# Stores of dK, dV and three weight gradients issued by ScalarE instead of GpSimd, in a decode layer's forward and backward pass

## The chip, the cores and the metric

The kernel runs on one core of a Trainium2 chip. The metric is the device time of one execution in microseconds (us); lower is better. A core has five engines that run instruction streams of their own: TensorE (PE in the profile), VectorE (DVE), ScalarE (ACT), GpSimd (POOL) and SyncE (SP). The last three can issue DMAs. An engine works through its stream in order, and an instruction that waits for a semaphore holds up all that stand behind it on its engine.

## The reference

One decode step of a transformer layer and all its gradients. There is one token of width 448. Attention has 16 heads of 256 over 8 groups of keys and values, and looks at the last 4096 of 32768 cached positions.

```
q = layernorm(x) @ wq;  k, v = the caches' last W = 4096 rows
p = softmax(q k^T / 16);  h = x + (p v) @ wo
g = layernorm(h) @ w_gate;  u = layernorm(h) @ w_up
out = h + (g * u) @ w_down
outputs: out, dx, dK, dV, dWq, dWo, dWg, dWu, dWd   (vjp with grad_out)
```

dK and dV have the shape of the whole caches, 8 x 32768 x 256 in bf16 each. All but the last 4096 rows of a group are zero, and these zeros must be written: 112 transfers of 2 MB.

## The kernel before

**Transfers.** SP loads `wq` and the first K window and then issues the 112 zero transfers (line 95, "the fills" below, numbered 1 to 112 in SP's order). Each writes the tile `zeros` to 2048 KB of `out_2` or `out_3`. GpSimd issues everything else: the loads of K and V windows (line 72, 2048 KB each), of `wo`, `w_gate`, `w_up`, `w_down` and again `wq`, and all stores of results.

**Stages.** First, for each group g of 8: scores, softmax and moments (forward attention). Then the output projection, layer norm and the gated feed-forward part, forward and backward (lines 388 to 434), which needs `w_up` as its last load. Then `dh_bc` (line 439, a ScalarE copy) and the gradient of the attention's output (line 442). Then the backward loop over g (line 551). For each g VectorE and ScalarE turn V, by transposes, into `dp`, and 16 chunks of two matmuls each (line 593) are cast from PSUM into the two 2 MB buffers `stg[0]` (dV, by ScalarE) and `stg[1]` (dK, by VectorE); line 598 stores both. There are five such buffers, `STG`, used in turn, so that a buffer of group g is free when a store of two or three groups earlier has landed.

**Weight gradients.** `outer` (line 469) multiplies rows on VectorE into a home buffer and stores it (line 474). It is called for dWg and dWu (`width` 896, 1568 KB each) right after the feed-forward backward, for dWd (`width` 448, so rows of 896 bytes, 1568 KB, home `Rt`), for dWo in two parts of 1792 KB (`width` 448, homes `Rt` and a slot of `S`), and for dWq in two parts of 2048 and 1536 KB (`width` 2048, after line 515 has reduced the reloaded `wq`). `Rt` is used in turn for dWu, the `w_down` load (line 490), dWd, the first part of dWo and the reloaded `wq`, and each of them waits until the store before it has left it.

**What sets the order.** The kernel is written in a tile language, and its planner puts the instructions of each engine in order and adds the semaphore waits. Every DMA of a hardware queue (SP, and ScalarE where it issues any) gets one of eight completion semaphores, the lanes, round and round in the planner's order over both engines; GpSimd's DMAs have eight lanes of their own. A DMA whose lane was used before waits, at issue, until the lane's DMA before it has landed. In the kernel before SP alone uses the hardware lanes: fill 50, for instance, waits for fill 42, and so on to the end, so that eight fills are under way at any time.

Of the kernel before, what the change touches and what calls it, by code (L numbers as in the profile page):

```python
# [13 lines left out]
D = 448  # L14
# [4 lines left out]
W = 4096  # L19
T = 32  # L20
F = 1792
FC = 14
Sk = 32768
# [19 lines left out]
def kernel(  # L43
        ctx, tc, A_x, A_k_cache, A_v_cache, A_wq, A_wo, B_x, B_w_gate, B_w_up, B_w_down, grad_out,
           out_0, out_1, out_2, out_3, out_4, out_5, out_6, out_7, out_8):
    nc = tc.nc
    V_, S_, P_ = nc.vector, nc.scalar, nc.tensor
    FILL = nc.sync
    IO = nc.gpsimd

    const = ctx.enter_context(tc.tile_pool(name="const", bufs=1))
    small = ctx.enter_context(tc.tile_pool(name="small", bufs=2))
# [12 lines left out]
    def slot_kv(k):  # L65
        return S[:, k, :].rearrange("p (t d) -> p t d", d=Dh)
# [4 lines left out]
    def load_window(dst, cache, g, q=None):  # L71
        (q or IO).dma_start(out=dst, in_=cache[0, g, Sk - W:, :].rearrange("(p t) d -> p t d", t=T))

# [3 lines left out]
    def load_V(g):  # L77
        load_window(Vw[g], A_v_cache, g)

    def flat_rows(w):  # L80
        return w.rearrange("a b -> (a b)").rearrange("(p x) -> p x", p=128)


    x_bf = const.tile([1, D], bf16, tag="rowa", name="x_bf")
    IO.dma_start(out=x_bf[:], in_=A_x.rearrange("a b d -> (a b) d"))
    go_bf = const.tile([1, D], bf16, tag="rowb", name="go_bf")
    IO.dma_start(out=go_bf[:], in_=grad_out.rearrange("a b d -> (a b) d"))
    wq_sb = S[:, 1:3, :].rearrange("p a b -> p (a b)")[:, 0:NI * HQ]
# [10 lines left out]
    wd0 = S[:, 3, 0:FC * D].rearrange("p (c n) -> p c n", n=D)  # L99
    IO.dma_start(out=wd0, in_=B_w_down.rearrange("(c p) n -> p c n", p=128))  # L100

# [109 lines left out]
    def evac(out, in_):  # L211
        if evac_ctr[0] % 2 == 0:
            S_.copy(out=out, in_=in_)  # L213
        else:
            V_.tensor_copy(out=out, in_=in_)  # L215
        evac_ctr[0] += 1
# [68 lines left out]
    def softmax(g):  # L285
        s = sT[g]
        pmax = small.tile([128, 2], f32, tag="pmax")
        V_.reduce_max(out=pmax[:], in_=s[:].rearrange("p t h -> p h t"), axis=AX)
        mt = ps.tile([2, 128], f32, tag="tmp", bufs=1)
        P_.transpose(mt[:], pmax[:], ident_f[:])  # L290
        gmax = small.tile([2, 1], f32, tag="gmax")
        V_.reduce_max(out=gmax[:], in_=mt[:], axis=AX)
        gd = small.tile([2, 2], f32, tag="gd")
        V_.tensor_scalar(out=gd[:], in0=ident_f[0:2, 0:2], scalar1=gmax[:, 0:1], scalar2=-SCALE, op0=ALU.mult, op1=ALU.mult)
        nb = ps.tile([128, 2], f32, tag="tmp", bufs=1)
        P_.matmul(nb[:], lhsT=ones_f[0:2, :], rhs=gd[:], start=True, stop=True)
        nbias = small.tile([128, 2], f32, tag="nbias")
        V_.tensor_copy(out=nbias[:], in_=nb[:])
        e = small.tile([128, T, 2], f32, tag="e_f")
        sums = small.tile([128, 2], f32, tag="psums")  # L300
        for h in range(2):
            S_.activation(out=e[:, :, h], in_=s[:, :, h], func=ACT.Exp, bias=nbias[:, h:h + 1], scale=SCALE, accum_out=sums[:, h:h + 1])
        rs = small.tile([128, 2], f32, tag="rsum")
        V_.reciprocal(out=rs[:], in_=total(sums[:], 2)[:])
        pf = small.tile([128, T, 2], f32, tag="p_f")
        V_.tensor_tensor(out=pf[:], in0=e[:], in1=rs[:].unsqueeze(1).to_broadcast([128, T, 2]), op=ALU.mult)
        V_.tensor_copy(out=pT_all[:, g], in_=pf[:])
        p_f[g] = pf
# [52 lines left out]
    for g in range(G):  # L361
# [6 lines left out]
        if g == 7:  # L368
            load_V(7)
            IO.dma_start(out=woA, in_=wo_v[:, 0:16, :])  # L370
        softmax(g)
# [3 lines left out]
        if g == 0:  # L375

            t = ps.tile([128, D], f32, tag="tmp", bufs=1)
            P_.matmul(t[:], lhsT=ones_bf[0:1, :], rhs=go_bf[:], start=True, stop=True)
            S_.copy(out=dh2_bc[:], in_=t[:])
            for c in range(FC):  # L380
                V_.tensor_tensor_reduce(out=wd0[:, c, :], in0=wd0[:, c, :], in1=dh2_bc[:], scale=1.0, scalar=0.0,  # L381
                                        op0=ALU.mult, op1=ALU.add, accum_out=d_hh[:, c:c + 1])
    IO.dma_start(out=woB, in_=wo_v[:, 16:32, :])
    IO.dma_start(out=wg_sb, in_=flat_rows(B_w_gate))
# [84 lines left out]
    def outer(dst, n0, n1, src, scal, width, home):  # L469

        sb = home[:, 0:(n1 - n0) * width].rearrange("p (n c) -> p n c", c=width)
        for n in range(n0, n1):
            V_.tensor_scalar(out=sb[:, n - n0, :], in0=src(n), scalar1=scal[:, n:n + 1], scalar2=None, op0=ALU.mult)
        IO.dma_start(out=dst[:, n0:n1, :], in_=sb)

    o4 = flat_rows(out_4).rearrange("p (i c) -> p i c", i=NI)
    o5 = out_5.rearrange("(b p) n -> p b n", p=128)
# [34 lines left out]
    def dxn_part(home, i0, i1):  # L512
        w = wq2(home, i0, i1)
        for i in range(i0, i1):
            V_.tensor_tensor_reduce(out=w[:, i - i0, :], in0=w[:, i - i0, :], in1=dq_bc[:, i % 2, :], scale=1.0, scalar=0.0,  # L515
                                    op0=ALU.mult, op1=ALU.add, accum_out=Pq[:, i:i + 1])
        outer(o4, i0, i1, lambda n: dq_bc[:, n % 2, :], xf1, HQ, home)

    def dx_out():
# [6 lines left out]

    side = {
        0: [lambda: outer(o6, 0, NI, lambda i: bc2[0][:, i % 2, :], xf2, HF, wg_sb),
            lambda: outer(o7, 0, NI, lambda i: bc2[1][:, i % 2, :], xf2, HF, wu_sb), load_wd],
        1: [ffn_out],  # L530
        2: [lambda: outer(o8, 0, FC, lambda n: dh2_bc[:], hh, D, Rt)],
# [13 lines left out]
    def vt_buf():  # L545
        k = vt_ctr[0] % 2
        vt_ctr[0] += 1
        return VTb[:, k, :].rearrange("p (i h c) -> p i h c", i=4, h=2)

    kt_buf = vt_buf  # L550
    for g in range(G):
        if g in V_AGAIN:
            Vw[g] = slot_kv(V_AGAIN[g])
        dp = bps.tile([128, T, 2], f32, tag="dp")
        for q in range(8):
            tr = ps.tile([128, 4, 2, 128], bf16, tag="tr", bufs=2)
            for i in range(4):
                for dh in range(2):
                    P_.transpose(tr[:, i, dh, :], Vw[g][:, 4 * q + i, dh * 128:(dh + 1) * 128], ident_bf[:])  # L559
            xt = vt_buf()  # L560
            evac(xt, tr[:])
            for i in range(4):
                for dh in range(2):
                    P_.matmul(dp[:, 4 * q + i, :], lhsT=xt[:, i, dh, :], rhs=doT[:, 4 * g + dh:4 * g + dh + 3:2],  # L564
                              start=(dh == 0), stop=(dh == 1))
        for again, sl in V_AGAIN.items():
            if sl == g:
                load_window(slot_kv(sl), A_v_cache, again)
        pds = small.tile([128, T, 4], bf16, tag="pds")
        V_.tensor_copy(out=pds[:, :, 0:2], in_=pT_all[:, g])  # L570
        df = small.tile([128, T, 2], f32, tag="df")
        V_.tensor_tensor(out=df[:], in0=dp[:], in1=delta[:, 2 * g:2 * g + 2].unsqueeze(1).to_broadcast([128, T, 2]), op=ALU.subtract)
        V_.tensor_tensor(out=pds[:, :, 2:4], in0=df[:], in1=pT_all[:, g], op=ALU.mult)
        r_ps = ps.tile([128, 128], bf16, tag="tmp", bufs=1)
        P_.transpose(r_ps[:], pds[:].rearrange("p t r -> p (t r)"), ident_bf[:])
        rows = rowb[:, g % 2]
        V_.tensor_tensor(out=rows, in0=r_ps[:].unsqueeze(1).to_broadcast([128, 8, 128]), in1=mrow[:].unsqueeze(2).to_broadcast([128, 8, 128]), op=ALU.mult)
        R_ps = ps.tile([128, 2 * Dh], f32, tag="tmp", bufs=1)
        for k, (E, rr) in enumerate(((Ed, do_rows), (Eq, q_rows))):
            ex = small.tile([H, 32, 4], bf16, tag="ex")  # L580
            V_.tensor_copy(out=ex[:], in_=E[:, g, :].unsqueeze(1).to_broadcast([H, 32, 4]))
            P_.matmul(R_ps[:, k * Dh:(k + 1) * Dh], lhsT=ex[:].rearrange("h a r -> h (a r)"), rhs=rr[:], start=True, stop=True)
        R = small.tile([128, 2 * Dh], bf16, tag="R")
        S_.copy(out=R[:], in_=R_ps[:])
        sv = slot_kv(STG[(2 * g) % 5])
        sk = slot_kv(STG[(2 * g + 1) % 5])
        stg = [sv, sk]
        for c in range(T // 2):
            d_ps = bps.tile([128, 2, 2, Dh], f32, tag="d2", bufs=2)
            for i in range(2):  # L590
                t = 2 * c + i
                k, a = t // 8, t % 8
                P_.matmul(d_ps[:, i, :, :].rearrange("p w d -> p (w d)"), lhsT=rows[32 * k:32 * k + 32, a, :], rhs=R[32 * k:32 * k + 32, :],  # L593
                          start=True, stop=True)
            for w in range(2):
                evac(stg[w][:, 2 * c:2 * c + 2, :], d_ps[:, :, w, :])
        for w, o in ((0, out_3), (1, out_2)):
            IO.dma_start(out=o[0, g, Sk - W:, :].rearrange("(p t) d -> p t d", t=T), in_=stg[w])
        for job in side[g]:
            job()  # L600

# [29 lines left out]
```

## Time and profile before

| | us |
|---|---|
| median of 3 runs (813.37 to 813.43) | 813.39 |
| profiled execution, whole | 813.5 |
| profiled execution, span of the instructions | 811.7 |
| busy in the span: PE | 490.7 |
| busy: DVE | 388.0 |
| busy: ACT | 164.7 |
| busy: POOL | 37.4 |

336.57 MB are moved by DMA in the span, 415 GB/s on average. By queue: 240.66 MB on the hardware queue of SP (70.4% of the 16 DMA engines' time), 95.13 MB on the software queue of GpSimd (27.9%). Of the 280.59 MB written to memory, 235 MB are zeros.

The profile counts time from the start of the span. In a row of the timeline the columns are start, length in time, engine, line, operation, output and inputs, and how many instructions were merged (x49). What stands in brackets is the engine's idle time just before, and what ended it. "PEclk" is the clock that TensorE was granted, as a share of full speed.

### The profile page before, as it was taken

How to read it: one execution, taken by the hardware profiler on the slowest of the kernel's cores; microseconds unless marked ns; L12 is line 12 of the kernel's file. 1: busy time of each engine (PE TensorE's matmuls, PEld its weight loads, DVE VectorE, ACT ScalarE, POOL GpSimd, SP SyncE). 2: the span in 40 equal slices, each digit the busy share in tenths (PEclk: the TensorE clock that was granted, in tenths of full speed). 3: DMA queues.
4: the chain of work that ended last, by engine and by line, in shares of the span. 5: the costliest groups of instructions: out<-in, count | busy, mean ns of one | idle time of the engine just before them, and what ended most of it. 6: DMA issues, size and time to landing. Idle time of an engine off the chain costs nothing.

```text
span 811.7 us, 12304 instructions
## 1 busy us (share of the span) xinstructions
PE 490.7 (60%) x4950; PEld 285.9 (35%) x4991; DVE 388.0 (48%) x1179; ACT 164.7 (20%) x261; POOL 37.4 (5%) x67
## 2 busy tenths in 40 slices
PE   3795956797978839252359999958996200170000
PEld 3664653555655525030336444412551000110000
DVE  4276834665656636028754555548554133550000
ACT  0311020202112000001024535534553100040000
POOL 3000000000000000000100001001101000000000
PEclk9987887887979879655555555555555555555555
DMA  9999999999999999999999999999999999999992
GB/s 376 409 427 428 427 428 430 428 428 425 426 427 425 428 410 422 427 424 434 427 421 427 430 427 414 427 423 405 427 418 426 402 428 416 430 431 430 430 423 97
DMA packets 25385, 336.57 MB, mean 415 GB/s; under 512 B 2720, under 2 KB 2768, under 8 KB 5488
## 3 DMA queue, kind: packets, MB, share of 16 engines
q1 hardware_dynamic: 16416, 240.66, 70.4%
q0 software_dynamic: 8912, 95.13, 27.9%
q8 instruction: 39, 0.64, 0.3%
q14 instruction: 18, 0.15, 0.0%
HBM read 55.18 MB, written 280.59 MB: 414 GB/s over the span
## 4 chain that ended last, share of the span: by engine, by line
issue 38%; PE 20%; DMA 14%; DVE 10%; another core or an unknown queue 6%; ACT 2%; POOL 1%; POOLq 0%; SPq 0%; DVEq 0%; ACTq 0%
PE MT L324 5%; DMA out_dram<-S 4%; DMA Rt<-in_B_w_up_dram 4%; PE d_ps L593 3%; DMA S<-in_A_k_cache_dram 3%; PE tr L559 2%; DVE S L442 2%; DMA S<-in_A_v_cache_dram 2%; PE tr L268 2%; PE acc L331 1%; DVE Rt L515 1%; DVE S L381 1%; DVE Rt L430 1%; DVE S L515 1%
## 5 line engine op out<-in xcount | busy, mean ns | idle before, releaser
L593 PE MATMUL d_ps<-R,Mt 32*128 32x512 bf16 x256 | 124.8, 612 | 57.0 <-DVE S L215 56.3
L324 PE MATMUL MT<-Rt,S 128*128 128x512 bf16 x471 | 150.5, 399 | 0.1
L320 DVE TENSOR_SCALAR Rt<-S,pf 128x256 bf16<-128x256 bf16 x512 | 120.4, 285 | 55.8 <-PE acc L331 39.2
L215 DVE CAST S<-d_ps 128x512 bf16<-128x512 f32 x128 | 87.9, 690 | 70.8 <-ACT S L213 64.5
L213 ACT CAST S<-d_ps 128x512 bf16<-128x512 f32 x128 | 75.0, 586 | 131.6 <-PE d_ps L593 130.2
L327 PEld LDWEIGHTS <-S 128*128 128x128 bf16 x512 | 50.3, 100 | 77.1 <-DMA S<-in_A_v_cache_dram 13.6
L268 PE MATMUL tr<-ident_bf,S 128*128 128x128 bf16 x512 | 50.7, 251 | 39.1 <-DMA S<-in_A_k_cache_dram 32.0
L559 PE MATMUL tr<-ident_bf,S 128*128 128x128 bf16 x512 | 69.0, 305 | 1.2 <-ACT Mt L213 1.2
L331 PE MATMUL acc<-ones_bf,Rt 128*128 128x1 bf16 x1024 | 63.2, 164 | 1.6 <-issue 1.5
L593 PEld LDWEIGHTS <-Mt 32*128 32x128 bf16 x256 | 22.7, 113 | 111.8 <-issue 110.4
L327 PE MATMUL acc<-pT_all,S 128*128 128x2 bf16 x512 | 49.3, 165 | 16.2 <-DMA S<-in_A_v_cache_dram 13.3
L213 ACT COPY Rt<-tr 128x1024 bf16<-128x1024 bf16 x32 | 32.4, 1012 | 126.7 <-PE tr L268 76.2
L559 PEld LDWEIGHTS <-S 128*128 128x128 bf16 x512 | 48.1, 135 | 25.4 <-issue 25.4
L268 PEld LDWEIGHTS <-S 128*128 128x128 bf16 x512 | 37.4, 112 | 40.9 <-DMA S<-in_A_k_cache_dram 32.6
L331 PEld LDWEIGHTS <-Rt 128*128 128x128 bf16 x1024 | 47.1, 97 | 6.2 <-issue 6.1
L213 ACT COPY Mt<-tr 128x1024 bf16<-128x1024 bf16 x32 | 32.4, 1013 | 23.5 <-PE tr L559 22.2
L215 DVE COPY Mt<-tr 128x1024 bf16<-128x1024 bf16 x32 | 22.0, 687 | 22.5 <-PE tr L559 18.9
L324 PEld LDWEIGHTS <-S 128*128 128x128 bf16 x512 | 32.5, 98 | 0.0
L168 PE MATMUL t<-st,ones_f 128*128 128x2 f32 x4 | 1.2, 364 | 48.6 <-DVE st L199 48.6
L215 DVE COPY Rt<-tr 128x1024 bf16<-128x1024 bf16 x32 | 21.9, 686 | 17.0 <-PE tr L268 15.6
L564 PEld LDWEIGHTS <-Mt 128*128 128x128 bf16 x512 | 21.1, 109 | 24.7 <-issue 10.9
L343 ACT COPY Rt<-kb 128x512 f32<-128x512 f32 x8 | 4.7, 585 | 120.2 <-PE kb L341 100.2
(189 smaller groups left out, 435.6 us busy)
## 6 DMA issues: line engine op xcount, KB each, us to landing
out_dram<-zeros SPq DMA_DIRECT2D x112, 2048.0 KB, 51.9
out_dram<-S POOLq DMA_DIRECT2D x16, 2048.0 KB, 29.1
S<-in_A_v_cache_dram POOLq DMA_DIRECT2D x10, 2048.0 KB, 41.7
S<-in_A_k_cache_dram POOLq DMA_DIRECT2D x7, 2048.0 KB, 27.5
S<-in_A_wq_dram SPq DMA_DIRECT2D x1, 3584.0 KB, 12.9
S<-in_A_wo_dram POOLq DMA_DIRECT2D x2, 1792.0 KB, 30.9
out_dram<-Rt POOLq DMA_DIRECT2D x2, 1568.0 KB, 32.9
S<-in_A_k_cache_dram SPq DMA_DIRECT2D x1, 2048.0 KB, 23.2
```

The lines of the kernel that those rows point to most:

```text
L213: S_.copy(out=out, in_=in_)
L215: V_.tensor_copy(out=out, in_=in_)
L268: P_.transpose(tr[:, i, dh, :], Xw[:, 4 * q + i, dh * 128:(dh + 1) * 128], ident_bf[:])
L320: V_.tensor_scalar(out=pk[:, i, h, :], in0=K[:, t, :], scalar1=pf[:, t, h:h + 1], scalar2=None, op0=ALU.mult)
L324: P_.matmul(MT[:, hf, :], lhsT=Vv[:, t, hf * 128:(hf + 1) * 128], rhs=pk[:, i, :, :].rearrange("p h d -> p (h d)"), start=(t == 0), stop=( ...
L327: P_.matmul(acc[:, 2 * hf:2 * hf + 2], lhsT=Vv[:, t, hf * 128:(hf + 1) * 128], rhs=pT_all[:, g, t, :], start=(t == 0 and hf == 0), stop=(t ...
L331: P_.matmul(acc[:, 4 + 2 * h + dk:5 + 2 * h + dk], lhsT=pk[:, i, h, dk * 128:(dk + 1) * 128], rhs=ones_bf[:, 0:1], start=False, stop=(t == ...
L442: V_.tensor_tensor_reduce(out=wo_b(b), in0=wo_b(b), in1=dh_bc[:], scale=1.0, scalar=0.0, op0=ALU.mult, op1=ALU.add, accum_out=doT_f[:, b:b ...
L515: V_.tensor_tensor_reduce(out=w[:, i - i0, :], in0=w[:, i - i0, :], in1=dq_bc[:, i % 2, :], scale=1.0, scalar=0.0, op0=ALU.mult, op1=ALU.a ...
L559: P_.transpose(tr[:, i, dh, :], Vw[g][:, 4 * q + i, dh * 128:(dh + 1) * 128], ident_bf[:])
L564: P_.matmul(dp[:, 4 * q + i, :], lhsT=xt[:, i, dh, :], rhs=doT[:, 4 * g + dh:4 * g + dh + 3:2], start=(dh == 0), stop=(dh == 1))
L593: P_.matmul(d_ps[:, i, :, :].rearrange("p w d -> p (w d)"), lhsT=rows[32 * k:32 * k + 32, a, :], rhs=R[32 * k:32 * k + 32, :], start=True, ...
```

## The change

A third name, `ST`, for ScalarE's DMA queue. Of the stores, those of dK and dV (16 of 2048 KB), of dWg and dWu and of the two parts of dWq now are issued by ScalarE. The stores with rows of 896 bytes (dWd and both parts of dWo), the two small outputs and all of GpSimd's loads stay on GpSimd. Nothing is changed in what is computed.

```
@@ -47,6 +47,7 @@
     FILL = nc.sync
     IO = nc.gpsimd
+    ST = nc.scalar
@@ -471,7 +472,7 @@
         for n in range(n0, n1):
             V_.tensor_scalar(out=sb[:, n - n0, :], in0=src(n), scalar1=scal[:, n:n + 1], scalar2=None, op0=ALU.mult)
-        IO.dma_start(out=dst[:, n0:n1, :], in_=sb)
+        (IO if width == D else ST).dma_start(out=dst[:, n0:n1, :], in_=sb)
@@ -595,7 +596,7 @@
         for w, o in ((0, out_3), (1, out_2)):
-            IO.dma_start(out=o[0, g, Sk - W:, :].rearrange("(p t) d -> p t d", t=T), in_=stg[w])
+            ST.dma_start(out=o[0, g, Sk - W:, :].rearrange("(p t) d -> p t d", t=T), in_=stg[w])
```

The planner's order changes with it, and the built program shows how. The 20 ScalarE stores and the fills now take turns on the same eight hardware lanes. So some fills wait for a store (dV0 and dK0 are the stores of group 0, and so on):

```
fill    50   52   58   59   64   66   68   71     75   79   82   83   88   92   94
waits   dWg  dWu  dV0  dK0  dK1  dV2  dK2  dWq b  dK3  dK4  dV5  dK5  dK6  dV7  dK7
```

All other fills wait for an earlier fill. A ScalarE store in turn waits for the fill, or the store, before it on its lane: dV1 for fill 52, dV2 for 56, dV3 for 63, dV4 for 67, dV6 for 76, dK6 for 77, dV7 for 80. SP's order of the fills and, up to the last casts of group 0, the order of PE and VectorE are those of before. After that VectorE's order differs: all 14 multiplications of dWd now follow group 0's last cast in one run, and the first ten of dWo, which overwrite dWd in `Rt`, stand before the casts of group 1 (before the change: among those of group 3). The reduction of the first part of `wq` (line 515, four instructions) now stands just after group 1, before the change it stood in group 6. The `w_down` load on GpSimd (line 490) waits, as before, for dWu's store, which is now ScalarE's.

More of the change, by code (lines that the diff above doesn't have):

```diff
@@ L49 @@
     IO = nc.gpsimd
+    ST = nc.scalar
     const = ctx.enter_context(tc.tile_pool(name="const", bufs=1))
@@ L473, in outer @@
             V_.tensor_scalar(out=sb[:, n - n0, :], in0=src(n), scalar1=scal[:, n:n + 1], scalar2=None, op0=ALU.mult)
-        IO.dma_start(out=dst[:, n0:n1, :], in_=sb)
+        (IO if width == D else ST).dma_start(out=dst[:, n0:n1, :], in_=sb)
     o4 = flat_rows(out_4).rearrange("p (i c) -> p i c", i=NI)
@@ L597 @@
         for w, o in ((0, out_3), (1, out_2)):
-            IO.dma_start(out=o[0, g, Sk - W:, :].rearrange("(p t) d -> p t d", t=T), in_=stg[w])
+            ST.dma_start(out=o[0, g, Sk - W:, :].rearrange("(p t) d -> p t d", t=T), in_=stg[w])
         for job in side[g]:
```

## The prediction

> **What bounds the kernel now.** I read the slices of the span first, then the DMA busy share at the end, then who SP waits for, then GpSimd's and VectorE's timelines.
>
> ```profile
> DMA  9999999999999999999999999999999999999992
> GB/s 376 409 427 428 427 428 430 428 428 425 426 427 425 428 410 422 427 424 434 427 421 427 430 427 414 427 423 405 427 418 426 402 428 416 430 431 430 430 423 97
> ```
>
> The DMA engines are full in 39 of 40 slices at some 427 GB/s. The time is the bytes over that rate; compute matters only where it leaves the DMA engines without work.
>
> ```profile
> SPq L95 <- DMA out_dram<-zeros: 710.9, 104, 9.9
> ...
> 761.90 10.03 SPq L95 DMA_DIRECT2D out_dram<-zeros  x3
> ```
>
> SP's waits: 104 of 112 fills wait for the fill eight before, never longer than 9.9 us, so there is always stock. The second row is three fills issued one landing apart, with 0.33 us for the last issue: (10.03 - 0.33) / 2 = 4.85 us per 2048 KB. That is my unit.
>
> ```profile
> 5.17 305.49 SPq L95 DMA_DIRECT2D out_dram<-zeros  x49
> ...
> 310.33 54.66 SPq L95 DMA_DIRECT2D out_dram<-zeros  x9
> ...
> 387.34 0.45 DVE L473 TENSOR_SCALAR S<-S,xf 128x896 bf16<-128x896 bf16 x1
> ...
> 388.08 2.36 POOL L474 DMA_DIRECT2D out_dram<-S  x1 [60.39 <-DVE S L473]
> 390.62 0.53 POOL L474 DMA_DIRECT2D out_dram<-Rt  x1 [0.18 <-issue]
> ...
> 465.89 0.55 POOL L598 DMA_DIRECT2D out_dram<-S  x1 [51.27 <-ACT S L213]
> ...
> 732.92 0.54 POOL L598 DMA_DIRECT2D out_dram<-S  x1 [0.17 <-issue]
> ```
>
> The timelines of SP, VectorE and GpSimd. SP had issued fill 49 at 310.33. Nine fills from there (49 to 57) took 54.66 us; the ninth is let go by the landing of fill 49, at 310.33 + 54.66 - 0.33 = 364.7. The first result store, dWg, is issued only at 388.08, dV0 at 465.89, the last dK at 732.92. So the fills run far ahead of compute, and that lead is what fills the DMA engines.
>
> **The change, part by part.** *Lanes.* Fill 50 now waits for dWg's store, which doesn't exist before 388, and SP stands still behind it. Everything up to then is as before, so all released work is through at 364.7.
>
> (A) dWg's last multiplication ends at 387.34 + 0.45 = 387.8. SP's first DMA needs about 1.0 us from issue to first bytes (no bytes from 0.7 to 1.75 us, then 730 GB/s to 2.3, in the windows of the start), which I also take for ScalarE. First bytes at 388.8: 24.1 us idle. (B) dWg is 1568 KB, 3.7 us; landing and the start of fill 50 cost 0.4 + 1.0 = 1.4 us idle. Bytes again from 394.0.
>
> (C) dWu's store stands on ScalarE behind `dh_bc`'s copy (ends 394.3); its landing, near 403, releases fill 52. Released are now fills 50 to 57, dWu and the `w_down` load: 8 x 2.097 + 2 x 1.606 = 20.0 MB, at the 424 GB/s of this stretch 47.1 us, so dry at 441.1. Fill 58 waits for dV0. Compute to dV0 isn't changed in order and waits for no DMA that is late, so dV0 is issued at 465.9, bytes at 466.9: 25.8 us idle.
>
> (D) From here each group's stores release a few fills. Until dV2 the released work is eight fills (58 to 65), four stores, two V loads and one `wq` part (15 x 2.097 MB), dWd, two dWo parts and the other `wq` part (6.85 MB): 38.3 MB, at the 419 GB/s of 467 to 573 us 91.4 us. When does dV2 come?
>
> ```profile
> 466.33 0.81 DVE L473 TENSOR_SCALAR Rt<-dh_bc,hh 128x448 bf16<-128x448 bf16 x3
> ...
> 556.50 0.53 POOL L598 DMA_DIRECT2D out_dram<-S  x1 [26.55 <-ACT S L213]
> ...
> 585.02 0.54 POOL L598 DMA_DIRECT2D out_dram<-S  x1 [26.07 <-ACT S L213]
> ...
> 663.55 2.29 DVE L515 CUSTOM_DVE_ANT_0 Rt<-Rt,Mt 128x2048 bf16<-128x2048 bf16 x1 [29.02 <-DMA Rt<-in_A_wq_dram]
> ```
>
> dWd's 14 multiplications at 0.27 us end at 470.3. The ten of dWo behind them wait until dWd's store has landed; the nearest row is the `w_down` load of the same shape beside fills, 24.4 us, so 495 (bounds: 16.3 us, dWg's store, and 43.4, dWd's own before). Then ten multiplications, and a group of 28.5 us (585.02 - 556.50): dV1 near 526, where it was 495.5. Behind it stand 3.8 us of dWo, a wait of some 5 us for the reloaded `wq` (its slot is free when dWo's first part has left, and all work released by then, 10.6 units, is through by 520; two loads follow), four line-515 rows of 2.2 us and a group: 572, bytes at 573. So 573 - 466.9 - 91.4 = 15 us idle; at least 0, and with 43.4 us for dWd and ten more for `wq` 44.
>
> After dV2 the groups come every 22 to 28 us and bring 2 stores and 3 to 6 fills, 24 to 39 us of transfers: no more idling. Sum: 813.5 + 24.1 + 1.4 + 25.8 + 15 = 880. From the end: after dV2 remain 47 fills, 12 stores and 3584 KB of dWq, 60.75 units x 4.85 = 295 us, plus some 4 for the slower rate while compute runs (422 against 432 GB/s), the 1.6 us without bytes at the span's end and the 1.8 us that the execution has over its span: 573 + 295 + 4 + 1.6 + 1.8 = 875. The two differ by rates taken over different stretches; I take **877**. The profiled 813.5 is within 0.02% of the median.
>
> *ScalarE's issues.* No row shows one. SP's take 0.33 to 0.50 us, GpSimd's 0.53: 20 x 0.4 = 8 us on an engine busy 165 of 812, at most 0.8 us a group in the chain of casts. With every dK store ScalarE also waits for VectorE's last cast of the group (0.69 us), and behind it stand the next group's casts. Cost: nothing, as stock covers it from dV2 on; before dV2 1.5 us a group inside (D)'s bounds. The lane waits of the stores bind late (fill 76 is the 11th after dV2, due near 675, just when dV6 is ready): ScalarE then waits on a busy DMA, which costs no bytes.
>
> *GpSimd* loses 20 issues, 11 us of an engine busy 37; nothing waits for it. Its loads are no longer behind stores in its stream, which is why (D) lets V and `wq` come as early as their buffers are free. One is special: dWg's issue took 2.36 us, beside VectorE's multiplications, where others take 0.53. The Trainium skill, "SBUF — State Buffer", section "SBUF: two separate sides", warns that GpSimd's descriptors starve while VectorE holds the shared port, and that ScalarE's DMAs don't; by it the change gains that 1.8 us. Its page "DMA: Bandwidth & Descriptors", section "Issuing engines are not separate DMA queues", speaks against any larger gain: all issuers share the 16 DMA engines and another issuer only saves issue time. By that rule alone the time stays at 813; it has no price for SP standing still.
>
> **Rivals.** (1) *Faster.* With a queue of their own the stores leave sooner, compute ends before 733, and the tail shrinks: in the last 21 us the DMA share falls from 1.0 to 0.03, about 15 us of unused engine time, so 799 at best. It decides if SP never waits for an unborn store; against it stands fill 50, issued at 317 before. (2) *No change:* same bytes at the same rate, 813.5, if lanes were not shared in effect. Same evidence against. (3) *Less slow:* TensorE has 0.50 of its clock from 361 on and is busy 24.8 of the 25 us before dV0. If the idle DMA engines bring the clock back (it had 0.96 at 200 to 222 us), dV0 comes up to 20 us sooner and (C) and (D) shrink: 840 to 857. Nothing in the trace ties the clock to DMA. (4) *Worse:* dWd's store takes as long as dWo's second part (66.2 us) in the queue's crowd, or ScalarE blocked by a lane holds casts while SP is dry: 877 + 42 = 919.
>
> **How the numbers follow.** Forecast 0.78, rival 1 0.05, rival 2 0.03, rival 3 0.06, rival 4 0.08. The likeliest gives 877. Its bounds: (D) at 0 gives 862, less 4 for rates, 858; (D) at 44 gives 906. 858 to 906 holds the forecast, and 8 in 10. This kernel's measurement can't tell less than 0.2% from no change; faster 0.05, within 0.03, slower 0.92.
>
> **What would show it.** Right: DMA slices near 0 around 365 to 389 and 441 to 467; among SP's waits, long ones (24 us and more) for stores; the first store still near 388 and dV0 near 466; dV1 30 us later than before; some 102 us of fills alone after the last dK. Wrong: fill 58 issued before dV0 has landed, or a DMA line of nines throughout.

## The result and the profile after

| | before | after |
|---|---|---|
| median (us) | 813.41 (813.37 to 813.74, 4 runs) | 873.53 (871.43 to 875.21, 4 runs) |
| ratio, 95% interval | 1 | 1.0737 (1.0713 to 1.0761) |
| profiled execution, whole | 813.5 | 871.43 |
| its span | 811.7 | 869.6 |

The change costs 60 us. One execution of the experiments below, 880.15 us with dWo held back, was in a slower state and is left out of its median and ratio. Line numbers of the changed kernel are one higher than before (the fills are line 96, the stores lines 475 and 599). First the slices of the span: 40 slices of 21.7 us, with the granted TensorE clock, the DMA share and the rate. Below, a fill is "let go" when nothing it waits for holds it any more, a store is "born" when it is issued with its data ready, and a "hole" is a stretch in which the DMA engines have next to nothing to move.

```profile
PEclk9997968798797796655656555555555555555555
DMA  9999999999999999219927999689999999999999
GB/s 375 418 425 427 426 430 428 427 427 428 429 425 427 423 425 423 90 75 403 427 92 304 402 396 396 269 359 423 423 430 424 428 429 424 432 426 427 428 426 387
```

Before, the second row was nines but for the last slice. Now there are two holes, slices 17 and 18 (348 to 391 us) and 21 and 22 (435 to 478), and a dent at 26. After it the rate is that of before to the end, and the last slice has 387 GB/s where it had 97: what is lost in the holes is added behind, though not in full (the tail, below). The clock stays at 0.5 to 0.6 through the holes.

Who SP waited for (total us, times, longest):

```profile
SPq L96 <- DMA out_dram<-zeros: 443.3, 72, 12.4
SPq L96 <- DMA out_dram<-S: 296.7, 11, 67.4
SPq L96 <- DMA out_dram<-Rt: 10.4, 1, 10.4
```

Before, of these there was only the first row, 104 times. Now SP stood 12 times for a result store, 307 us in all, once 67.4 us: fill 50, until dWg had landed. ScalarE's timeline around the two long stops (the rows with ACTq are DMA issues):

```profile
385.16 0.37 ACTq L475 DMA_DIRECT2D out_dram<-S  x1
391.09 0.53 ACT L440 CAST dh_bc<-dh_ps 128x448 bf16<-128x448 f32 x1 [21.86 <-PE dh_ps L163]
391.17 0.34 ACTq L475 DMA_DIRECT2D out_dram<-Rt  x1
...
461.37 1.06 ACTq L599 DMA_DIRECT2D out_dram<-S  x2
```

dWg's store is issued at 385.16, dWu's behind `dh_bc`'s copy, and the first store of group 0 at 461.37. By their landings in the trace, fill 49 was through at 364.8, dWg at 391.0 (fill 50 is issued in the same moment, at 391.00), fill 57 at 441.6, dV0 at 467.7 (fill 58: 467.73). Both holes lie between the last fill that was let go and the store that the next one waits for. The windows put numbers on them. The columns are the window, its length, the busy us (and the number of instructions) of PE, of PE's weight loads, of DVE, ACT and POOL, then granted clock, DMA share (1.01 is full) and GB/s:

```profile
340.00:365.00 25.00, 13.01 (x147) 8.02 (x147) 6.32 (x29) 2.01 (x4) 0.00 (x0) 0.64 0.51 213
365.00:389.00 24.00, 7.46 (x32) 5.43 (x30) 21.08 (x52) 1.75 (x3) 0.00 (x0) 0.50 0.14 57
...
441.00:467.00 26.00, 25.81 (x159) 10.59 (x158) 15.18 (x31) 11.85 (x18) 0.00 (x0) 0.50 0.19 81
467.00:573.00 106.00, 71.17 (x599) 37.83 (x597) 58.31 (x117) 34.73 (x51) 6.20 (x8) 0.53 0.90 360
...
768.00:870.00 102.00, 0.00 (x0) 0.00 (x0) 0.00 (x0) 0.00 (x0) 0.00 (x0) 0.50 0.98 417
```

The third loss is the 0.90 of 467 to 573. Most of it lies just before dV2 (556 to 569: share 0.30), and what made dV2 late stands in VectorE's timeline:

```profile
494.38 2.55 DVE L474 TENSOR_SCALAR Rt<-dh_bc,oT_f 128x448 bf16<-128x448 bf16 x10 [19.10 <-DMA out_dram<-Rt]
```

The ten multiplications of dWo wait for dWd's store to leave `Rt`, and group 1's casts stand behind them: dV1 is issued at 525.37, before the change at 495.5. A run below tests this.

The losses can be closed over all 16 engines. From 340 to 573 the share is 0.71, so 68 of 233 us were without work (before the change: none). The tail from 768 to the end has 0.99, before it had 0.64 over 43.7 us: 1 us without work for 16. That is 53 of the 58 us by which the profiled execution grew; the other 5 are not accounted for.

### The profile page after: what moved, and what is told of

Its sections match the earlier page's. It is cut to its first block, busy times and chain, and to the rows that moved or that the text cites. A ratio compares the mean times of both kernels' runs of the same rounds, so it can differ in the third digit from the quotient of the medians.

```text
span 869.6 us, 12268 instructions
## 1 busy us (share of the span) xinstructions
PE 487.2 (56%) x4991; PEld 281.9 (32%) x4991; DVE 389.0 (45%) x1179; ACT 164.3 (19%) x261; POOL 24.7 (3%) x47
## 3 DMA queue, kind: packets, MB, share of 16 engines
q10 hardware_dynamic: 2880, 40.44, 11.0%
## 4 chain that ended last, share of the span: by engine, by line
PE 26%; issue 22%; DMA 20%; DVE 10%; ACT 2%; POOL 0%; SPq 0%; ACTq 0%; POOLq 0%; DVEq 0%
PE d_ps L594 7%; DMA out_dram<-zeros 5%; PE MT L325 5%; PE tr L560 5%; DMA Rt<-in_B_w_up_dram 4%; DMA out_dram<-Rt 3%; DMA out_dram<-S 3%; DMA S<-in_A_k_cache_dram 3%; DVE S L443 2%; DMA S<-in_A_v_cache_dram 2%; PE tr L269 2%; PE dp L565 2%; DMA Rt<-in_A_wq_dram 1%; DVE S L216 1%; PE acc L332 1%
## 5 line engine op out<-in xcount | busy, mean ns | idle before, releaser
L325 PE MATMUL MT<-Rt,S 128*128 128x512 bf16 x512 | 160.1, 400 | 0.0
L594 PE MATMUL d_ps<-R,Mt 32*128 32x512 bf16 x256 | 122.7, 612 | 64.4 <-DVE S L216 64.4
L328 PEld LDWEIGHTS <-S 128*128 128x128 bf16 x512 | 50.2, 100 | 75.8 <-DMA S<-in_A_v_cache_dram 12.3
L269 PE MATMUL tr<-ident_bf,S 128*128 128x128 bf16 x512 | 51.2, 252 | 40.4 <-DMA S<-in_A_k_cache_dram 33.3
L560 PE MATMUL tr<-ident_bf,S 128*128 128x128 bf16 x512 | 64.1, 292 | 3.8 <-DVE Mt L216 3.6
L560 PEld LDWEIGHTS <-S 128*128 128x128 bf16 x512 | 45.2, 130 | 21.7 <-issue 21.7
L269 PEld LDWEIGHTS <-S 128*128 128x128 bf16 x512 | 37.8, 112 | 42.2 <-DMA S<-in_A_k_cache_dram 33.8
L325 PEld LDWEIGHTS <-S 128*128 128x128 bf16 x512 | 32.5, 98 | 0.0
L274 PE MATMUL sT<-qT,Rt 128*128 128x2 bf16 x512 | 23.0, 166 | 9.1 <-DVE Rt L216 7.7
```

The lines of the kernel that those rows point to most:

```text
L269: P_.transpose(tr[:, i, dh, :], Xw[:, 4 * q + i, dh * 128:(dh + 1) * 128], ident_bf[:])
L274: P_.matmul(out_ps[:, 4 * q + i, :], lhsT=xt[:, i, dh, :], rhs=vecT[:, 4 * g + dh:4 * g + dh + 3:2], start=(dh == 0), stop=(dh == 1))
L325: P_.matmul(MT[:, hf, :], lhsT=Vv[:, t, hf * 128:(hf + 1) * 128], rhs=pk[:, i, :, :].rearrange("p h d -> p (h d)"), start=(t == 0), stop=( ...
L328: P_.matmul(acc[:, 2 * hf:2 * hf + 2], lhsT=Vv[:, t, hf * 128:(hf + 1) * 128], rhs=pT_all[:, g, t, :], start=(t == 0 and hf == 0), stop=(t ...
```

## The experiments

Twelve more kernels were run: some move a part of the 20 stores, some change the fills, and the last four ("order hint") change the planner's order. A "gate" is a fill that waits for a store. Times are medians with the ratio to the kernel before and its 95% interval.

| kernel | us | ratio |
|---|---|---|
| dK and dV alone moved | 872.40 | 1.0727 (1.0708 to 1.0746) |
| dWg, dWu, dWq alone moved | 845.27 | 1.0387 (1.0372 to 1.0403) |
| a small piece of each store moved | 874.80 | 1.0767 (1.0733 to 1.0802) |
| dK of the last group alone moved | 845.08 | 1.0385 (1.0353 to 1.0417) |
| groups 6 and 7 alone moved | 846.70 | 1.0407 (1.0389 to 1.0424) |
| changed kernel, dWo held back | 864.33 | 1.0629 (1.0595 to 1.0662) |
| changed kernel, fills on GpSimd | 913.58 | 1.1228 (1.1212 to 1.1245) |
| changed kernel, fills of 4 MB | 878.42 | 1.0796 (1.0780 to 1.0812) |
| order hint 42 | 868.96 | 1.0690 (1.0671 to 1.0709) |
| order hint 55 | 814.89 | 1.0030 (1.0018 to 1.0043) |
| order hint 90 | 905.07 | 1.1120 (1.1104 to 1.1136) |
| order hint 55 on four loads | 814.34 | 1.0014 (1.0004 to 1.0025) |

**Is it the bytes on ScalarE's queue, or the lanes?** One piece of each store goes over ScalarE, the rest stays with GpSimd. The edit for dK and dV is shown; the stores of `outer` are split in the same way.

```
-            ST.dma_start(out=o[0, g, Sk - W:, :].rearrange("(p t) d -> p t d", t=T), in_=stg[w])
+            d3 = o[0, g, Sk - W:, :].rearrange("(p t) d -> p t d", t=T)
+            ST.dma_start(out=d3[:, T - 1:T, :], in_=stg[w][:, T - 1:T, :])
+            IO.dma_start(out=d3[:, 0:T - 1, :], in_=stg[w][:, 0:T - 1, :])
```

> Each of the 20 moved stores is split: its last row (1/7 of a dWg or dWu store, 1/4 or 1/3 of dWq's, 1/32 of a dK or dV store) goes over ScalarE, the rest over GpSimd as before the change. So nearly all store bytes travel as they did before (16 dK and dV stores: 31/32 of them), and only the lanes are shared. In the built order fill 50 waits for dWg's piece, 51 for dWu's, 56 for dV0's, 59 and 60 for dV1's and dK1's, 62 for dV2's: 55 fills before dV0, against 57 in the changed kernel. My theory: slower than the changed kernel. Idle 21 us before dWg; then 6 fills, dWg, dWu and w_down, 8.3 units, dry near 427, idle 35 us to dV0 at 462; some 12 and 5 us more before dV1 and dV2: 813.4 + 21 + 35 + 17 = 887, range 876 to 898. Rival (the bytes on ScalarE's queue, or the rate of that queue, are what costs): with most bytes back on GpSimd the time falls back to 813 to 820.

It took 874.8, below the expected range by 1 us. ScalarE's queue in that kernel (packets, MB, share of the 16 engines' time):

```profile
q10 hardware_dynamic: 2880, 2.56, 0.9%
```

In the changed kernel q10 carried 40.44 MB. With a sixteenth of that the loss is the same, so the bytes and the rate of ScalarE's queue are not its cause. The loss is differently made up: the hole before dV0 is longer (30 us, 434.0 to 464.2, share 0.01), and the third loss is gone (467 to 573: share 1.01), since dV1 was issued at 493 (changed kernel: 525). Against my sum (35 and 17 us) that is 22 us less idle time, but the time is only 12 us under it. So my sum of holes doesn't add up to this time, and the other 10 us stay open.

**Does each stop have a price?** Two kernels undo a part each.

```
-        (IO if width == D else ST).dma_start(out=dst[:, n0:n1, :], in_=sb)
+        IO.dma_start(out=dst[:, n0:n1, :], in_=sb)
```

> Only the 16 stores of dK and dV go to ScalarE; dWg, dWu and dWq go back to GpSimd. Fills 50 and 52 are free again; the built order has fill 57 wait for dV0, 58 for dK0, 62 and 63 for dV1 and dK1, 67 for dV2. My theory (a lane shared with SP's fills stops SP at a store that is not born): what counts is how many fills are let go before dV0, 56 here and 57 in the changed kernel, so taking away the first two stops saves nothing: the idle time only moves into one stretch. Seven fills (50 to 56), dWg, dWu and the w_down load are 9.3 units of 4.85 us behind 364.8, dry near 410, first bytes of dV0 near 462: 50 us idle, and some 8 us more before dV1. 813.4 + 50 + 8 = 871, range 864 to 878. Rival A (each stop has a price of its own, so those of dWg and dWu are saved): 873.5 - 21.4 - 1.4 = 851, range 845 to 855. Rival B (a store costs because ScalarE issues it, 60 us over 20 stores): 813.4 + 16 x 3 = 861.

872.4, as my theory had it: without the stops at dWg and dWu nothing is saved. Fill 56 landed at 402.5, dV0 was issued at 463.6, and from 410 to 462 the DMA share was 0.08: some 60 us without work from 389 to 462 (0.45 over the first 21 us) in place of two holes. Rivals A (851) and B (861) fall.

```
-            ST.dma_start(out=o[0, g, Sk - W:, :]....
+            IO.dma_start(out=o[0, g, Sk - W:, :]....
```

> Only dWg, dWu and the two parts of dWq go to ScalarE (4 of the 20 stores); dK and dV go back to GpSimd. In the built order fill 50 waits for dWg, 52 for dWu, 77 for the first part of dWq and 80 for the second. My theory: the DMA engines idle from 364.8 to 386 as in the changed kernel, then run without a break, since 25 fills (52 to 76) are free; but dWq stands in group 6 here, near 660, and the fills up to 76 with all other released transfers (some 47.5 units from 391 on) are through near 624, so SP stands a second time, 25 to 36 us. 813.4 + 21.4 + 1.4 + 26 = 862, range 848 to 875. A long wait of SP for a dWq store should show, 25 us or more. Rival A (only the first stops cost): 836. Rival B (price per ScalarE store, 3 us each): 825.

845.27: 17 us under my value, 3 under my range and 9 over rival A's. Rival B (825) falls. Who SP waited for:

```profile
SPq L96 <- DMA out_dram<-Rt: 119.7, 2, 109.8
```

SP stood 109.8 us at fill 77, as expected, but the DMA engines ran low only from 625 to 640 (share 0.66): dWq was born at 641.5 and not at 660, because stores and loads land sooner when fewer fills are beside them (the reload of `wq`'s first part took 19.6 us, in the kernel before 51.9). So the second stop cost some 5 us, and by its time alone this run does not separate me from rival A. The length of a stop is not its price: 109.8 us of standing left some 5 us without work.

**One store, and the latest ones.** If only the order of births counts, even the last store must cost. This edit and the next are made in the kernel before, not in the changed one.

```
-            IO.dma_start(out=o[0, g, Sk - W:, :]....
+            (ST if g == G - 1 and w == 1 else IO).dma_start(out=o[0, g, Sk - W:, :]....
```

> One store alone goes to ScalarE: dK of the last group, the last of the 20 to be born. In the built order fill 83 waits for it (before the change SP issued fill 83 at 536). My theory: SP stands at fill 83 until dK7 has landed, whenever that is; after it come 30 fills, dK7 and about dV7, 32 x 4.85 = 155 us, and 3.4 us around. dK7 came at 733 in the kernel before, at 679 in the kernel with four weight-gradient stores moved; between them, with the DMA engines free from about 650, I take 703: 861, range 845 to 885, and SP shows one wait of 100 us or more for a store. Rival A (a price per ScalarE store, 60 us over 20): 816. Rival B (only stores that stand early, where the DMA engines have little stock, cost): 813.

```profile
DMA  9999999999999999999999999999877159999999
```

```profile
SPq L96 <- DMA out_dram<-S: 155.2, 1, 155.2
```

One store of 2 MB out of 235 MB of zeros and 20 stores costs 31 us (845.08). SP stood once, 155.2 us, and the hole now lies where that store is born: dK7 was issued at 681.1, landed at 692.1, and 30 fills and what lies around them followed: 692.1 + 1.0 + 30 x 4.85 + 3.4 = 842, against 843.9 of the profiled execution. My time of birth (703) was 22 us too late, which is why the time lies at the lower edge of my range; the rest held. Rivals A and B (816 and 813) fall.

```
-            IO.dma_start(out=o[0, g, Sk - W:, :]....
+            (ST if g >= 6 else IO).dma_start(out=o[0, g, Sk - W:, :]....
```

> Only the four stores of groups 6 and 7 (dV6, dK6, dV7, dK7) go to ScalarE. In the built order fill 75 waits for dV6, 76 for dK6, 82 for dV7, 84 for dK7. My theory: after dV6 remain 38 fills, four stores and dWq, 43.75 x 4.85 = 212 us; dV6 came at 669 before, at 633 in the kernel with four weight-gradient stores moved: 633 to 669 + 212 + 4 = 849 to 885, I take 865. So four of the latest stores cost nearly what all 20 do. Rival A (price per store): 825. Rival B (only early stops cost): 813.

846.7, 2 us under the range: dV6 was born at 627, before the earliest time that I took. Four late stores cost 33 us, half of what all 20 do; 627 + 212 + 4 = 843 by the sum of the expectation. Rivals A (825) and B (813) fall.

**VectorE's order, the third loss.**

```
+    def hold():
+        z32 = small.tile([128, 32], f32, tag="z32")
+        V_.tensor_scalar(out=z32[:], in0=last["df"], scalar1=0.0, scalar2=None, op0=ALU.mult)
+        V_.tensor_tensor(out=oT_h[:], in0=oT_f[:], in1=z32[:], op=ALU.add)
...
-        3: [lambda: outer(o5, 0, 16, lambda n: dh_bc[:], oT_f, D, Rt)],
+        3: [hold, lambda: outer(o5, 0, 16, lambda n: dh_bc[:], oT_h, D, Rt)],
```

> The changed kernel with VectorE's multiplications for dWo held back until group 3 (by two small VectorE instructions that add 0 x a value of group 3 to their factors; the results stay the same). So dV1 no longer stands behind dWd's store and dWo: dV1 near 497, dV2 near 530. The gates of SP up to fill 64 stay as they are (50 dWg, 52 dWu, 58 dV0, 59 dK0, 64 dK1), then 68 dK2. My theory: the idle stretches before dWg and dV0 stay (21 + 1 + 21 us), the third loss, before dV1 and dV2 (11 to 15 us), goes: 813.4 + 44 = 858, range 854 to 866. Rival (the third loss is not VectorE's order but the stops at 64 and 66 themselves): 873.

```profile
467.00:530.00 63.00, 55.04 (x480) 28.95 (x478) 38.81 (x90) 27.81 (x41) 6.05 (x6) 0.55 1.01 410
530.00:573.00 43.00, 11.98 (x107) 7.34 (x107) 15.42 (x21) 5.40 (x9) 1.11 (x2) 0.50 1.01 412
573.00:700.00 127.00, 91.58 (x372) 30.43 (x371) 74.88 (x119) 52.66 (x87) 0.51 (x1) 0.50 0.97 409
```

In the trace the multiplications of dWo now run behind group 1's last casts (at 502.6), dV1 came at 501, and the stretch that had 0.90 is full. The ratio fell by 0.011, some 9 us; 4 us of the gain went again behind 573 (0.97, where the changed kernel had 1.01). There VectorE waited for the reloaded `wq` until 556.7 (changed kernel: 533.6), with group 2's last casts behind it, and dV2 came at 562, not at 530. So the third loss is VectorE's order, about 10 us, as long as fills 64 and up wait for the stores that it delays. The rival (873) falls. The three executions lie between 862.0 and 868.0, so the size is known to a few us only.

**More bytes in each fill.**

```
-            for i in range(NZ):
-                FILL.dma_start(out=reg[i], in_=zeros[:])
+            for i in range(0, NZ, 2):
+                m = min(2, NZ - i)
+                FILL.dma_start(out=reg[i:i + m].rearrange("n p f -> p n f"), in_=zeros[:].unsqueeze(1).to_broadcast([128, m, ZW]))
```

> The changed kernel with the fills in pieces of 4 MB (three of 4 MB and one of 2 MB per region: 64 fills for 112), read from the same tile twice. A fill let go now carries twice the bytes, so the eight lanes hold nearly twice the lead. In the built order fill 31 waits for dWu, 35 for dV0, 42 for the second part of dWq: 60 units of 2 MB are let go before dV0 (57 in the changed kernel), 72 before dWq b (70 there). My theory: about 2 us idle before dWg (53 units are free of it, 49 before), 3 to 5 around dWu, 27 before dV0, up to 8 later: 813.4 + 40 = 853, range 843 to 866. Rival A (the size of a fill does not matter): 873. Rival B (a loss per stop of SP, 11 stops for 15): 857, which this run cannot tell from my value, but the idle stretches can: theirs shrink alike, mine only before dWg.

It missed: 878.42, 12 us over the range and slower than the changed kernel. By its time alone rival A (873) lies nearest. By the windows the size of a fill does matter, but in both directions: from 340 to 394 the share is 0.61 (changed kernel: 35 us without work, here 21), and a new hole appears later. SP's waits for stores were up to 104.6 us long.

The larger stock also stands in the way of the transfers that compute waits for. `w_up` landed at 367.9 (changed kernel 359.0), so dWg came at 394.1 (385.2); the load of the second part of `wq` was issued at 587.8 (554.6), so dV2 came at 601.3 (568.2), and dWq's second part, for which fill 42 waits, landed only at 623.7: a fourth hole, share 0.82 from 573 to 700. I had moved the fills in my sum and left the births where they were.

**The other queue for the fills.** GpSimd's lanes are its own, so fills on GpSimd cannot wait for a store of ScalarE.

```
-    FILL = nc.sync
-    IO = nc.gpsimd
+    FILL = nc.gpsimd
+    IO = nc.sync
...
-    FILL.dma_start(out=wq_sb, in_=flat_rows(A_wq))
-    load_K(0, FILL)
+    IO.dma_start(out=wq_sb, in_=flat_rows(A_wq))
+    load_K(0, IO)
```

> The changed kernel with the other two queues swapped: GpSimd issues the 112 fills alone, SP issues all loads and the stores of dWd and dWo; ScalarE keeps its 20 stores. Now the fills have GpSimd's eight lanes to themselves and no fill waits for a store; the stores and loads share the hardware lanes. VectorE's order is that of the changed kernel. My theory: SP's lost lead was all the loss, so it is gone: 813, range 803 to 824, with the DMA slices full throughout. Rival A (the stores from ScalarE or VectorE's changed order cost by themselves): 835 or more. Rival B (fills over GpSimd's queue are fed too slowly, its issue beside VectorE took up to 2.36 us): above 824 with gaps spread over the whole span.

913.58: slower than all others and 90 us over my range, so it did not separate my theory from rival A. The slices and the packet line:

```profile
DMA  8999999999999999999999999999993671815455
...
DMA packets 36064, 336.57 MB, mean 369 GB/s; under 512 B 2596, under 2 KB 16168, under 8 KB 16168
```

The fills ran without a break (share 1.01 from 300 to 600), all were issued by 659, and the engines then starved behind a late compute. So rival B, fills fed too slowly by GpSimd, falls. The two loads of `wo`, 34.7 and 26.2 us over GpSimd in the changed kernel, took 90.3 and 133.3 us over SP. On SP's queue the 896-byte rows are packets of their own: the trace has 13,572 packets of 896 bytes there (`wo`, both loads of `w_down`, dWd and dWo have 4096 + 3584 + 1792 + 4096 = 13,568 rows, and the four single rows of x, grad_out, out and dx make up the rest), where GpSimd's queue in the kernel before carried packets of 4480 bytes, five rows each. If each row takes turns with one 16 KB packet of a fill (median 611 ns, the row's 41 ns), a load of `wo` takes 2048 / 16 x 0.652 = 83 us, an estimate near the 90 but far from the 133; it was not tested by itself.

**The order alone.** If only the order in which fills and stores take the lanes costs, then a mere hint to the planner must give the loss back. It leaves every DMA on its queue. The edge below puts one load behind fill 55 in the planner's order and adds no wait on the chip (the load is issued at 326.7, that fill at 344.3; `fill_ins` is the list of the fills); the planner then counts all later compute, and its stores, some 19 fills later.

```
...
-            IO.dma_start(out=woA, in_=wo_v[:, 0:16, :])
+            la = IO.dma_start(out=woA, in_=wo_v[:, 0:16, :])
+            tc.add_manual_dep(la.ins, fill_ins[54].ins.name,
+                              mybir.DependencyInfo(mybir.DependencyClass.NoSync, mybir.DependencyReason.DATA), reason="order")
```

> The changed kernel, all 20 stores on ScalarE, with one hint to the planner and nothing else: in its order the first load of wo shall stand behind fill 55 (an order without a wait; nothing on the chip waits for it). The planner then places every later store some 19 fills later among the fills, about where the fills really are when the store is born. In the built order fill 69 waits for dWg (changed kernel: 50), 70 for dWu, 78 for dK0, 81 for dV1, 85 for dV2, 107 for dK6, 111 for dV7; dWg's store in turn waits for fill 55, dV0's for 64, dV6's for 95. In the kernel before SP issued fill 69 at 436, 78 at 493, 85 at 554, 107 at 738, 111 at 767; the stores landed at 404 (dWg), 492 (dK0), 715 (dK6), 747 (dV7). My theory (only the order in which fills and stores take the lanes costs): no stop of SP empties the DMA engines, and the loss is gone though ScalarE issues all 20 stores: 813, range 808 to 823, DMA slices full throughout. ScalarE waits up to 40 us for a lane near dV6, which costs nothing. Rival (ScalarE's queue, its issues or VectorE's changed order cost by themselves): 830 or more.

814.89, with all 20 stores on ScalarE: 59 of the 60 us are gone, and the rival (830 or more) falls. But the DMA engines were not full throughout, as I had expected (slices of 20.4 us; the profiled execution took 817.56):

```profile
DMA  9999999999999999999999999788989999999998
```

From 510 to 612 the share is 0.86, 14 us without work. They cost nothing, because the tail has lost its own idle time: 0.96 over the last 47.8 us, where the kernel before had 0.64 over 43.7, 16 us. After a hole the engines run out of work together (see the last section), so a hole of some 15 us is paid for by the tail, as far as this account goes.

The same edge behind fill 42 and fill 90:

> The same hint, smaller: the first load of wo behind fill 42. Fill 56 waits for dWg, 57 for dWu, 65 for dK0, 68 for dV1, 72 for dV2, 75 and 77 for dWq. My theory: no idle time before dWg (fills to 55 last until 394), 14 us before dV0, 20 before dV1, 0 to 5 later: 813.4 + 37 = 850; by dV2 at 570 and the 54.75 units left, 841. I take 846, range 834 to 858. Rival (the loss has nothing to do with the order): 873.

> The same hint, far too large: the first load of wo behind fill 90. Now no fill waits for an unborn store in time that matters (fill 104 for dWg), but dWg's store waits for fill 90 to land, and ScalarE's casts stand behind it. With no store beside them the fills land every 4.85 us from 411 (fill 57) on: fill 90 near 571. My theory: dWg's store at 571 where it was ready at 388, dV0 near 649, the DMA engines run out of fills near 680, the groups follow at 20 to 30 us each: dK7 near 828, end near 838, range 815 to 868, and the idle time lies at the end of the span. Rival (the waits of ScalarE for lanes cost nothing, as I argued for the changed kernel): 813.

With 42 the time was 868.96, 11 us above the expected range and nearer to the rival's 873, so by its time alone it doesn't speak for the order. The reason is a side effect that all three kernels of this kind have: the planner now issues the first part of `wo` last of its four loads, at 326 instead of 287, it lands at 380, and dWg comes 39 us later (424.2 for 385.2). That eats what six or seven more released fills (29 to 34 us) give: by dV2, at 594.6, and 54.75 units left, 594.6 + 1.0 + 266 + 3.4 = 865, against 868.4 profiled. So the sum from the one store that binds held, and my input to it was wrong. With 55 the same 39 us cost next to nothing: more fills were let go, and the tail paid for what was missing.

With 90 the loss is on the other side. ScalarE's waits and the slices:

```profile
ACT dh_bc L443 <- DMA out_dram<-zeros: 156.8, 1, 156.8
```

```profile
DMA  9999999999999999999999999999999821815454
```

dWg's store stood on ScalarE until a fill had landed, 156.8 us, with `dh_bc`'s copy and all casts behind it. dWg was issued at 565.8 (expected 571) and dV0 at 638 (649); the groups then took longer than I had them (dV1 68 us after dV0), and the end is 905, not 838 and 37 us over the range. So the rival, that ScalarE's waits cost nothing, falls: they cost nothing only while compute has slack.

The last kernel gives an edge to all four loads, the first behind fill 55 and each other behind the load before it, so that they keep their order (`hint` adds the edge; three of its four calls are shown):

```
+    hint(IO.dma_start(out=woB, in_=wo_v[:, 16:32, :]))
+    hint(IO.dma_start(out=wg_sb, in_=flat_rows(B_w_gate)))
+    hint(IO.dma_start(out=wu_sb, in_=flat_rows(B_w_up)))
```

> The hint of 55 once more, but given to all four loads that stand there (both parts of wo, w_gate, w_up, in this order), so that GpSimd issues them in the order of the changed kernel; with the hint on the first load alone the planner had put it last, and all compute behind it came 37 us later. Gates as with the hint of 55 (69 dWg, 70 dWu, 77 and 78 dV0 and dK0, 83, 85, 87, ... 111 dV7). My theory: dWg's store issued near 394 (its lane is fill 55, which landed at 394 in the kernel before), dV0 near 470, no empty stretch of the DMA engines: 813.5, range 812 to 816, no difference from the kernel before. What is left over it is the price of ScalarE's issues themselves. Rival (ScalarE's stores have a price of their own, as the 0.3% of the run with the hint on one load could mean): 815 to 820.

```profile
DMA  9999999999999999999999999999969999999996
```

```profile
SPq L97 <- DMA out_dram<-zeros: 608.5, 85, 19.3
SPq L97 <- DMA out_dram<-S: 96.4, 7, 36.6
```

814.34 (1.0004 to 1.0025): 0.3 to 2.0 us over the kernel before, about the 0.2% that the prediction took as the least that can be told. dWg is issued at 394.4, as expected. SP still stands for stores, seven times and up to 36.6 us, and the released work outlasts most of these stops. The dent is a hole before dV2 (issued at 599.8): from 570 to 612 the share is 0.78, 9 us without work, and again the tail pays (0.86 over the last 44.6 us, 6 us for 16). VectorE's order is that of the changed kernel here too: the multiplications of dWo wait 22.6 us for dWd's store, and dV1 comes at 533.9, later than in the changed kernel. So that order costs nothing by itself. No kernel here beats the kernel before.

## Why the prediction was right, point by point

The forecast was 877, the median 873.53, and the mechanism was the one forecast. 877 was taken between two sums: the one by parts (880) was 9 us above the profiled time, the one from the end (875) 4 us.

- *Lanes.* Right, and shown by itself: a sixteenth of the bytes on ScalarE costs as much, one store alone costs 31 us, and the order alone gives 59 of the 60 us back. What the prediction did not say is that the stops are not additive. dK and dV alone cost as much as all 20, since what counts is how many bytes are let go before a store is born.
- *(A) 24.1 us.* From fill 49's landing (364.8, predicted 364.7) to dWg's first bytes (issue 385.16 + 1.0): 21.4. dWg came 2.9 us sooner, as `w_up` landed at 358.96 for 361.62 with fewer fills beside it. The prediction took "as before" where the missing fills had already begun to act.
- The engines were empty earlier than I counted: the window 340 to 365 has a share of 0.51, and in steps of 5 us 1.03, 0.91, 0.45, 0.10 and 0.05. The slowest engine had work until 364.8, others ran dry from 345 on. That is the unevenness that stood in the tail of the kernel before (0.63 over 768 to 812); after the holes the engines are level and the tail has 0.98. Taken to the slowest engine's end, as the prediction did, it is counted once.
- *(B) 1.4 us.* dWg landed at 390.99, fill 50 was issued at 391.00, as forecast; from dWg's last bytes to the fill's first (390.0 to 391.8, share 0.03) it is 1.8 us. The 0.4 us taken from the last bytes to the landing was a little small.
- *(C) 25.8 us.* From fill 57's landing (441.6; predicted 441.1) to dV0's bytes (461.37 + 1.0): 20.8. dV0 came 4.5 us before its time in the kernel before. 2.9 us of that are (A)'s; the rest coincides with a clock of 0.57 from 394 to 441, where it was 0.50 before the change. An unchanged order was taken for an unchanged time, which was not quite so.
- *(D) 15 us.* dV1 at 525.4 (predicted 526), dV2 at 568.2 (572), dWd's store 25.6 us (24.4 taken). The share of 0.90 over 106 us is 10.6 us idle, and the kernel with dWo held back gives 9 of them back. Mechanism right, size 4 us too large.
- *The two sums.* With the measured parts, 813.5 + 21.4 + 1.4 + 20.8 + 10.6 = 868, 4 us under the profiled 871.43; from the end, dV2's first bytes at 569.2 and the predicted 295 + 4 + 1.6 + 1.8 make 871.6. The second sum is the better one: it needs no holes, only dV2's birth, and that was forecast within 4 us (572, measured 568.2). In the first, (A), (C) and (D) were together 12 us too large.
- *ScalarE's issues.* 0.34 to 0.37 us for most (0.4 taken), 1.2 for the longest, and hidden: the last kernel pays at most 2 us for all 20. dWg's issue of 2.36 us on GpSimd is 0.37 on ScalarE; these 2 us, too, bring nothing here. That ScalarE's waits for lanes cost nothing was right here (dK6, held until fill 77 landed at 680.0) and is wrong in general: the hint of 90.
- *Rivals.* (1) falls twice: SP does wait, and with the waits harmless the stores still bring no gain (814.3). Here the Trainium skill's page "DMA: Bandwidth & Descriptors", section "Issuing engines are not separate DMA queues", holds: it says that the DMAs of all issuers run on the same 16 engines and that a further issuer saves only issue time. The 60 us come on top of what it says. (3) did not occur: through the holes the clock is 0.50 (rows of 365 to 389 and 441 to 467). It was higher than before only at 345 to 355 (0.83 and 0.85, before 0.64 and 0.70), as the engines ran dry, and from 394 to 441, where they were full; what raised it is not shown. (2) and (4) are excluded by the time.
- *What would show it.* The holes are where they were put, dV1 is 29.9 us later. One item was wrong: after dK7's landing (727.1) fills ran alone for 141 us, not 102. The 102 doesn't follow from the prediction's own rows either: five groups of 22 to 28 us behind a dV2 of 572 would bring dK7 near 682 to 712. It doesn't touch the end, which is set by dV2 and the bytes left.

## What to carry to other kernels

Before a DMA is moved to another issuing engine, look at what the moved transfer and the long stream of the other issuer share: here eight completion lanes, given out in the planner's order. If that order is early, the stream stands until the moved store is born; if it is late, the store stands until the stream has passed. The price is read from one store, the one that binds: its time of birth plus the bytes not yet let go over the rate. With the measured birth put in, this came within 4 us of the profiled time in four kernels here. A stop is free as long as the released work lasts longer than it, and a short hole can be free too, if the engines would otherwise have run dry unevenly at the end. One store in the wrong place is enough to cost 31 us.

## What was not expected of the hardware

- 2 MB loads and stores land faster when fewer fills are under way: dV0's store took 6.3 us in the changed kernel and 16.3 us before, dWo's second part 12.2 and 66.2. dV7 was issued at 702.9, before at 732.2, though dV1 was 30 us late. How much of this gain is the faster loads and how much VectorE's other order was not separated.
- The DMA engines drift apart under a full load. The trace has 16 completions of each fill, taken here as one per engine. In the kernel before those of fill 1 lie between 33.0 and 34.6, those of fill 49 between 341.6 and 364.6, with 14 of them before 351. In the changed kernel those of fill 50, after the hole, lie within 0.2 us. Which engine is slow, and why, was not looked into.
- A row of 896 bytes travels as a packet of its own on SP's queue and in larger packets on GpSimd's (896 bytes against 4480; `wo`'s loads at 90 and 133 us for 35 and 26). That speaks for leaving these rows with GpSimd, as the change does; their stores from ScalarE were not tried.
- Open: the 0.3 to 2.0 us that remain in the last kernel, the 10 us that the sum of holes misses in the kernel with small pieces, and how much of the slow `wo` loads in the kernel with GpSimd's fills is the size of the packets and how much the queue before them.
